# First chunks of the four sequences as one group with the decay in the mask, layer 1 opened on three of them, and squares moved to ScalarE

## The chip, the cores and the metric

The kernel runs on one core of a Trainium2 chip. The metric is the device time in microseconds (us) of one execution, of which a profile records the span from the first to the last instruction. Most executions of one kernel agree within about 0.3%, but some run with a lower granted TensorE clock in the records. So runs marked slow are left out of the ratios.

Engine names as in the profile: PE is TensorE, PEld its weight loads (they overlap PE), DVE is VectorE, ACT is ScalarE, POOL is GpSimd (here it issues the loads and scales v), SP is SyncE. A name with a q, such as POOLq, is the engine's sequencer.

## The reference

A decayed linear attention is followed by a feed-forward layer. There are 4 sequences of 768 positions, 8 heads of width 64, model width 512 and hidden width 2048; inputs are float32.

```python
gamma = 1.0 - 2.0 ** (-5.0 - np.arange(H))          # one decay per head
for t in range(S):
    state = gamma * state + outer(k[:, :, t], v[:, :, t])
    y[:, :, t] = scale * (q[:, :, t] @ state)
x = y.transpose(0, 2, 1, 3).reshape(B * S, H * D)   # 3072 x 512
h = x @ w_in                                        # layer 1
g = h + sin(alpha * h) ** 2 / (alpha + 1e-9)
out = g @ w_out                                     # layer 2
```

## The kernel before

Positions are cut into 24 chunks of 128, six per sequence. A chunk's attention has three stages. T transposes q and k on PE and copies them out of PSUM. A makes the scores and multiplies them by a 0/1 mask. M makes the values: for the first chunk of a sequence from the scores alone, for later ones also from a running state, which M updates too. The decay is taken out of the scores: v is scaled by a growing factor per position (`kg`), and the result by a falling one (`qg`, one table per chunk position, made by `decay_table`).

Chunks are put in groups for the feed-forward layer. Layer 1 has 16 slices per group: 4 matmuls, a sine on ScalarE, a square on ScalarE ("A") or VectorE ("D"), and on VectorE the sum `g`, which frees the slice's PSUM bank. A phase weaves layer 1 of one group with layer 2 of the group before and the attention of the group after.

```python
groups = [3, 2, 4, 4, 4, 4, 3]                 # chunks in the order of the sequences
def stage_T(j):
    open_T(j); half_T(j, 0); half_T(j, 1)      # 8 transposes on PE
    nc.scalar.copy(st["qkT", j], st["pt", j])  # 128x1024 from PSUM, on ScalarE
def stage_A(j):
    ...                                        # 8 matmuls into pa
    nc.vector.tensor_mul(aT, pa, mask_bc)      # 128x1024
def stage_M(j):
    ...                                        # state part (c > 0), value part, state update
    nc.vector.tensor_mul(xT[g][:, :, o:o + C], py, qg[:, c])
    ...                                        # two ScalarE copies of the state
def ff_in(g, f, square):
    ph = psum.tile([128, n], F32, tag="mm", bufs=4)
    ...                                        # 4 matmuls
    nc.scalar.activation(out=s, in_=ph, func=Sin, scale=alpha_sb[:, f:f + 1])
    ...                                        # square on ScalarE or VectorE
    return lambda: nc.vector.scalar_tensor_tensor(gT[g][:, f, :], s, rec_alpha[:, f:f + 1], ph, ...)

phase(0, [], {2: [G(3)], 5: [G(4)], 9: [T(3), V(3)], 11: [A(3)], 13: [G(5)]}, "AAD")
...                                            # chunk 4, and part of layer 2 of group 0
phase(1, outs[8:], {7: [T(5), V(5)], ...}, "AAAD")
for g in range(2, NG):
    ...
    phase(g, out_pieces(g - 1), att, "AAD" if g == 2 else "AAAD")
```

All loads but alpha and the first q and k go through one queue on POOL, in the order chunk 0 (v), 1, 2, three w_in pieces, chunk 3, w_in, chunk 4, four w_out pieces, then the other chunks. `idle_work` are matmuls on zeros, put where PE has nothing to do and meant to keep its clock up.

## Time and profile before

The kernel took 234.36 us in the median of 3 runs (234.17 to 234.95). The profiled execution spans 233.0 us.

These lines are from the page of the kernel before: the busy times (us, share of the span, instructions), the shares of the chain of waits, and two groups of instructions (out<-in, shapes, count | busy us, mean ns of one | idle us before it).

```profile
span 233.0 us, 4372 instructions
PE 214.8 (92%) x1737; PEld 113.8 (49%) x1766; DVE 146.8 (63%) x233; ACT 167.9 (72%) x297; POOL 84.4 (36%) x99
...
PE 72%; DVE 16%; ACT 7%; issue 3%; DVEq 0%; ACTq 0%
...
L224 DVE TENSOR_TENSOR s<-s 128x512 f32<-128x512 f32 (+2 forms) x30 | 19.5, 651 | 9.4 <-ACT s L220 9.4
...
L161 ACT COPY qkT<-pt 128x1024 bf16<-128x1024 bf16 x21 | 21.0, 1000 | 0.7 <-PE pt L154 0.7
```

PE is the bound over the span, but not everywhere. The timeline of PE of the kernel before (start us, duration us, then what it waited for in brackets) shows where layer 1 of groups 0, 1 and 2 starts:

```profile
17.45 3.55 PE L217 MATMUL ph<-xT,w_in 128*128 128x384 bf16 x20 [0.24 <-DVE xT L202]
...
39.26 0.60 PE L217 MATMUL ph<-xT,w_in 128*128 128x256 bf16 x4 [0.66 <-DVE xT L202]
...
64.55 1.02 PE L217 MATMUL ph<-xT,w_in 128*128 128x512 bf16 x3 [0.81 <-DVE xT L202]
```

And this is the busy time of the engines in two stretches of the kernel before (columns: stretch, its length, busy us of PE, PEld, DVE, ACT and POOL with instructions, granted clock, DMA engines' share, GB/s):

```profile
24.00:39.00 15.00, 11.02 (x121) 6.52 (x121) 13.50 (x23) 11.28 (x22) 6.83 (x9) 1.00 1.59 192
...
94.00:228.00 134.00, 131.96 (x954) 67.02 (x970) 75.59 (x103) 96.68 (x160) 7.30 (x8) 1.00 0.19 44
```

From 94 us on PE is 98% busy (131.96 of 134.00), and a shorter operation elsewhere can win next to nothing. From 24 to 39 us VectorE is 90% busy and PE 73%.

### The profile page before, as it was taken

The numbers are of one execution on the slowest core, as the hardware profiler recorded it, in microseconds if no ns is written. First come the engines' busy times: TensorE is split into PE (matmuls) and PEld (weight loads), VectorE is DVE, ScalarE is ACT, GpSimd is POOL, SyncE is SP. The second block draws the span as 40 slices with busy tenths as digits, with TensorE's granted clock in tenths as the row PEclk, the third lists the DMA queues.
The fourth block names the chain that finished last, engine by engine and source line by source line (L and its number), as shares of the span: only waits on it lengthen the run. The fifth ranks groups of instructions, "written<-read, shape, count | busy, mean of one in ns | idle before, by whom it ended". The sixth has DMA issues, their size and how long they took to land.

```text
span 233.0 us, 4372 instructions
## 1 busy us (share of the span) xinstructions
PE 214.8 (92%) x1737; PEld 113.8 (49%) x1766; DVE 146.8 (63%) x233; ACT 167.9 (72%) x297; POOL 84.4 (36%) x99
## 2 busy tenths in 40 slices
PE   7998867988889998999999999999999999999992
PEld 3554435555545454445555454455445545555440
DVE  6695996578846799646656656576557575445400
ACT  5478984787868886787787786786787876777420
POOL 8964734987999999930000000000000000000000
PEclk9999999999999999999999999999999999999998
DMA  9999999999999999970110110110111011111111
GB/s 131 141 197 184 184 207 171 155 150 184 114 153 108 111 147 113 141 88 3 48 45 0 48 45 1 48 45 1 48 45 45 3 45 45 48 45 45 45 71 67
DMA packets 82612, 20.48 MB, mean 88 GB/s; under 512 B 75408, under 2 KB 79520, under 8 KB 82592
## 3 DMA queue, kind: packets, MB, share of 16 engines
q0 software_dynamic: 77024, 13.37, 76.4%
q1 hardware_dynamic: 5568, 6.83, 8.5%
q8 instruction: 14, 0.23, 0.4%
q14 instruction: 6, 0.05, 0.1%
HBM read 27.27 MB, written 6.29 MB: 144 GB/s over the span
## 4 chain that ended last, share of the span: by engine, by line
PE 72%; DVE 16%; ACT 7%; issue 3%; DVEq 0%; ACTq 0%
PE po L234 31%; PE ph L217 27%; DVE aT L172 5%; DVE gT L225 4%; PE scratch L274 4%; ACT s L220 3%; PE pt L154 3%; PE pa L169 3%; DVE xT L202 3%; ACT qkT L161 3%; DVE s L224 2%; PE py L186 2%; PE py L190 2%; ACT s L222 1%; DVE qg L130 1%
## 5 line engine op out<-in xcount | busy, mean ns | idle before, releaser
L225 DVE SCALAR_TENSOR_TENSOR gT<-s,rec_alpha,ph 128x512 bf16<-128x512 f32 (+2 forms) x112 | 74.2, 669 | 52.3 <-ACT s L222 51.2
L217 PE MATMUL ph<-xT,w_in 128*128 128x512 bf16 (+2 forms) x444 | 99.5, 348 | 6.0 <-DVE gT L225 3.5
L234 PE MATMUL po<-w_out,gT 128*128 128x512 bf16 x361 | 95.4, 379 | 2.2 <-issue 1.4
L220 ACT ACTIVATE s<-ph,alpha_sb 128x512 f32<-128x512 f32 (+2 forms) x112 | 69.8, 626 | 36.1 <-PE ph L217 35.0
L217 PEld LDWEIGHTS <-w_in 128*128 128x128 bf16 x448 | 43.6, 98 | 51.6 <-issue 8.7
L234 PEld LDWEIGHTS <-gT 128*128 128x128 bf16 x384 | 34.7, 98 | 33.4 <-issue 0.5
L222 ACT ACTIVATE s<-s 128x512 f32<-128x512 f32 (+2 forms) x82 | 46.6, 568 | 2.6
L172 DVE TENSOR_TENSOR aT<-pa,mask 128x1024 bf16<-128x1024 f32 x24 | 29.3, 1222 | 6.7 <-PE pa L169 6.6
L224 DVE TENSOR_TENSOR s<-s 128x512 f32<-128x512 f32 (+2 forms) x30 | 19.5, 651 | 9.4 <-ACT s L220 9.4
L71 POOL DMA_DIRECT2D vr<-in_v_dram x24 | 21.9, 913 | 3.9 <-DMA w_out<-in_moe_w_out_dram 1.7
L71 POOL DMA_DIRECT2D qr<-in_q_dram x23 | 21.3, 927 | 3.3 <-DMA w_out<-in_moe_w_out_dram 1.7
L71 POOL DMA_DIRECT2D kr<-in_k_dram x23 | 20.4, 889 | 4.7 <-DMA w_out<-in_moe_w_out_dram 3.2
L161 ACT COPY qkT<-pt 128x1024 bf16<-128x1024 bf16 x21 | 21.0, 1000 | 0.7 <-PE pt L154 0.7
L243 ACT COPY o_sb<-po 128x512 f32<-128x512 f32 x23 | 13.5, 590 | 8.1 <-PE po L234 8.1
L206 ACT CAST s_bd<-ps 64x256 bf16<-64x256 f32 x40 | 14.5, 363 | 5.6 <-PE ps L199 4.1
L202 DVE TENSOR_TENSOR xT<-py,qg 128x512 bf16<-128x512 f32 x24 | 16.3, 679 | 2.5 <-PE py L190 2.5
L146 POOL TENSOR_TENSOR vr<-vr,kg 128x512 bf16<-128x512 bf16 x15 | 16.2, 1083 | 3.9 <-ACT s L222 2.1
L274 PE MATMUL scratch<-warm 128*128 128x512 bf16 x35 | 11.5, 462 | 1.4 <-DVE warm L105 1.2
L169 PE MATMUL pa<-qkT 64*128 64x128 bf16 x192 | 9.5, 219 | 2.3 <-ACT qkT L161 2.0
L169 PEld LDWEIGHTS <-qkT 64*128 64x128 bf16 x192 | 5.4, 94 | 11.5 <-ACT qkT L161 5.7
L190 PE MATMUL py<-aT,vr 128*64 128x128 bf16 x192 | 9.5, 220 | 0.5 <-DVE xT L202 0.4
L154 PE MATMUL pt<-ident,qr 128*128 128x128 bf16 x92 | 8.9, 219 | 1.0 <-DVE xT L202 1.0
(53 smaller groups left out, 89.2 us busy)
## 6 DMA issues: line engine op xcount, KB each, us to landing
out_dram<-o_sb SPq DMA_DIRECT2D x24, 256.0 KB, 2.0
vr<-in_v_dram POOLq DMA_DIRECT2D x24, 128.0 KB, 5.3
qr<-in_q_dram POOLq DMA_DIRECT2D x23, 128.0 KB, 4.9
kr<-in_k_dram POOLq DMA_DIRECT2D x23, 128.0 KB, 5.1
w_in<-in_moe_w_in_dram POOLq DMA_DIRECT2D x4, 512.0 KB, 10.2
w_out<-in_moe_w_out_dram POOLq DMA_DIRECT2D x4, 512.0 KB, 12.1
q<-in_q_dram SPq DMA_DIRECT2D x1, 256.0 KB, 3.3
k<-in_k_dram SPq DMA_DIRECT2D x1, 256.0 KB, 4.1
```

The lines of the kernel that those rows point to most:

```text
L71: nc.gpsimd.dma_start(out=t, in_=chunk_of(src, j))
L161: nc.scalar.copy(st["qkT", j], st["pt", j])
L169: nc.tensor.matmul(pa[:, e, p, :], qkT[r, NP + p, :], qkT[r, p, :], start=(p == 0), stop=True, skip_group_check=True)
L172: nc.vector.tensor_mul(aT.rearrange("p e n t -> p (e n) t"), pa.rearrange("p e n t -> p (e n) t"), mask_bc)
L202: nc.vector.tensor_mul(xT[g][:, :, o:o + C], py, qg[:, c])
L217: nc.tensor.matmul(ph, w_in[:, i, f * 128:(f + 1) * 128], xT[g][:, i, :], start=(i == 0), stop=(i == KS - 1))
L220: nc.scalar.activation(out=s, in_=ph, func=ACTF.Sin, scale=alpha_sb[:, f:f + 1])
L222: nc.scalar.activation(out=s, in_=s, func=ACTF.Square)
L224: (nc.vector if square == "D" else nc.gpsimd).tensor_mul(s, s, s)
L225: return lambda: nc.vector.scalar_tensor_tensor(gT[g][:, f, :], s, rec_alpha[:, f:f + 1], ph, op0=ALU.mult, op1=ALU.add)
L234: nc.tensor.matmul(po[g, ts], gT[g][:, f, ts * C:(ts + 1) * C], w_out[:, f, :], start=(f == 0), stop=(f == FF - 1))
L274: nc.tensor.matmul(scratch[:, :w], warm[:, :128], warm[:, :w], start=True, stop=True)
```

## The change

The intent has four parts.

1. The first chunks of the four sequences (called e0 to e3 here) make up group 0. They need no state, and with the decay put into the mask (`dec`, eight exponentials and one product) also no scaled v and no `qg` before M: M ends in a plain ScalarE copy.
2. Layer 1 opens on three of them: the first 8 slices run on 384 columns, then e3 is worked in, the same 8 slices run on its 128 columns, and slices 8 to 15 run on all 512.
3. The order of the queue changes: e3 comes after the first two w_in pieces, and the w_out pieces, which all stood behind w_in and chunks 3 and 4, now alternate with the last two of w_in.
4. From phase 1 on, all squares go to ScalarE, and the transposed copies of all later chunks go from ScalarE to VectorE.

The diff, cut to its core:

```diff
-    groups = [3, 2, 4, 4, 4, 4, 3]
+    order = [b * NCH for b in range(B)]
+    order += [b * NCH + c for b in range(B) for c in range(1, NCH)]
+    sizes = [4, 2, 4, 4, 4, 4, 2]
 ...
+    load_chunk(0, "v"); load_chunk(order[1]); load_chunk(order[2])
+    load_w_in(0); load_w_in(1); load_chunk(order[3])
+    load_w_out(0); load_w_in(2); load_w_out(1); load_w_in(3); load_w_out(2); load_w_out(3)
 ...
+    for h in range(H):
+        nc.scalar.activation(out=dec[:, h % 2, h // 2, :], in_=tio, func=ACTF.Exp, scale=lng[h], bias=back[:, h:h + 1])
 ...
-        nc.scalar.copy(st["qkT", j], st["pt", j])
+        nc.vector.tensor_copy(st["qkT", j], st["pt", j])
 ...
+        if c == 0:
+            nc.scalar.copy(x, py)
+            return
 ...
+    n3, early = 3 * C, 8
+    for f in range(early):
+        ff_in(0, f, "AAD"[f % 3], (0, n3))()
+    half_T(e3, 0, nc.scalar); idle_work(2); half_T(e3, 1, nc.vector); idle_work(4)
+    stage_A(e3)
+    decay_table(1); scale_v(e0, nc.vector); idle_work(4)
+    for f in range(4):
+        ff_out(0, 0, f)
+    stage_M(e3); idle_work(3)
+    for f in range(early):
+        ff_in(0, f, "AD"[f % 2], (n3, 4 * C))()
+    for t in s_bd:
+        nc.vector.memset(t, 0.0)
+    phase(0, [...], {9: [G(2)], 10: [G(3)], 12: [G(4)], 14: [G(5)]}, "AAD", range(early, FF))
 ...
-        phase(g, out_pieces(g - 1), att, "AAD" if g == 2 else "AAAD")
+        phase(g, out_pieces(g - 1, range(sizes[g - 1])), att, "A")
```

## The prediction

> **What bounds it now.** The chain of waits is 72% PE; PE is busy 92% of the 233.0 us span. Busy PE is not useful PE, so I count columns: a 512-column matmul runs every 0.216 us, a 384-column one every 0.162 us; one chunk's attention costs PE about 1.46 us (transposes 0.44, scores 0.33, state product 0.25, value product 0.22, state update 0.22). Useful work sums to about 199 us (estimate); the lost 34 us lie, by the timeline: 13.3 us before the first layer-1 matmul (17.45 us), 6.8 up to 39.3 (phase 0), 4.3 up to 64.6 (phase 1), 2.2 in phase 2, about 2.3 in the PE-bound rest, 4.1 after the last matmul (228.8). The change touches only what comes before the rest; it moves almost no PE work, so only those losses count.
>
> **Head.** It removes the v scaling, the state products and both state copies from the first three chunks, but adds eight exponentials (0.32 us each) and a 1.22 us mask product. ScalarE then carries copies, qg (4 x 0.32), the 1.28 us table load and the last x copy (0.6). First layer-1 matmul: 15.9 us instead of 17.45. It cannot be much earlier: POOL's waits show the first w_in piece landing near 15.6, and its place in the queue is unchanged.
>
> **Phase 0, the doubtful part.** Eight slices on three chunks are ScalarE-bound (1.03 us with the square there, 0.52 without): done near 24. The fourth chunk then runs serially (copy, scores, 1.22 us mask, values, copy): its layer 1 starts near 28.5, with ScalarE and PE nearly idle. Eight 128-column slices cost VectorE about 0.49 us each (estimate 0.34 per g, 0.30 per square): to 33.5. The last eight slices have 512 columns: VectorE pays 8 x 0.70, three squares 0.68, four decay tables 0.68 and two memsets 0.55, about 11 us; last g near 44.6, and PE, done near 42, waits for it. In the data queue w_out3 lands near 36 (each weight piece 2.55 us, each chunk 2.6), so no weight is late.
>
> **Fill and phase 1.** From 45 to 57 dense PE work covers chunks 4 and 5. Transposed copies go to VectorE: the Trainium skill ("VectorE: DVE Perf Modes", "Why PSUM operands drop a tier") allows 2 elements a cycle for 16-bit data from PSUM, so I estimate 0.69 us against ScalarE's 1.00; no copy of this form is in the trace. Phase 1 (256 columns, four chunks' attention) is VectorE-bound: 16 x 0.45 + 4 x (0.69 + 1.22 + 0.68) = 17.6, ScalarE about 18 with every square; 18.7 us with coupling, against 14.5 of PE work. Phase 2 starts near 75.8 instead of 64.6, but with only 8.4 us more work done.
>
> **Rest.** All squares on ScalarE make it 26 us per 33 us phase: still hidden. PE work left 151 us, losses 4.4, tail 4.1: span 235.5.
>
> **Predicted:** 236.5 us (timed runs are 1.4 above the span), range 232 to 240; faster by over 2% 0.1, within 2% 0.76, slower 0.14.
>
> **What would show it.** First layer-1 matmul near 15.9; a stretch of 24 to 29 us with little useful PE; VectorE busy over 90% from 34 to 44 with PE waiting for g; phase 1 about 19 us with VectorE above 90%; PE over 97% after 100 us; transposed copies 0.69 us.
>
> **What would make it wrong.** A faster phase 0 (VectorE operations overlapping, the fourth chunk's chain hidden): up to 5 us better. Phase 2 with less waste since POOL and VectorE collide less (one 1.67 us square at 91 us). Worse: late weights or chunks, or all ScalarE squares delaying g in phases 1 and 2.

## The result

The changed kernel took 237.63 us in the median of 4 runs (237.24 to 238.37), against 234.66 us (234.17 to 235.37) for 4 runs of the kernel before. The ratio is 1.0128, with a 95% interval of 1.009 to 1.0167. Ratios here are the mean time of one kernel's fast runs over that of the other's in the same rounds, so not quite the ratio of the medians. The change is slower, by 1.3%, within the 2% that counts as the same. The profiled span went from 233.0 to 235.5 us.

The same parts of the page of the changed kernel; the squares on VectorE are down to nine, and are not among the larger groups any more:

```profile
span 235.5 us, 4500 instructions
PE 214.7 (91%) x1769; PEld 115.2 (49%) x1798; DVE 142.7 (61%) x233; ACT 168.1 (71%) x327; POOL 92.6 (39%) x107
...
PE 64%; POOL 17%; DMA 12%; DVE 2%; issue 2%; ACT 1%; POOLq 0%
...
L190 DVE COPY qkT<-pt 128x1024 bf16<-128x1024 bf16 x20 | 13.8, 689 | 7.9 <-PE pt L180 7.5
```

Two things are to be seen. The transposed copy fell from 1000 ns on ScalarE to 689 ns on VectorE. And the chain of waits now puts 29% on POOL and on loads, which had no such share before. That is a strong hint, and the experiments show that it misleads.

The starts of layer 1 of groups 0, 1 and 2 in the timeline of PE of the changed kernel:

```profile
15.69 2.11 PE L258 MATMUL ph<-xT,w_in 128*128 128x384 bf16 x12
...
59.20 0.60 PE L258 MATMUL ph<-xT,w_in 128*128 128x256 bf16 x4
...
77.09 1.02 PE L258 MATMUL ph<-xT,w_in 128*128 128x512 bf16 x4 [0.33 <-DVE xT L243]
```

At the third of these the two kernels can be compared, but not directly: the changed kernel has one more chunk done by then. A chunk is 64 matmuls of 128 columns in layer 1 (3.46 us at the pace of 0.216 us per 512 columns), 16 matmuls of 512 columns in layer 2 (3.46 us), and 0.99 us of transposes, scores and values. In turn its order has put off one state product and one state update: counted in the traces, 48 and 56 matmuls of these stand before that point, against 56 and 64 in the kernel before, which is 0.47 us less. That makes 7.4 us more done (estimate; the prediction says 8.4). So:

| | before | changed | difference |
|---|---|---|---|
| layer 1 of group 0 starts, us | 17.45 | 15.69 | -1.8 |
| layer 1 of group 2 starts, us | 64.55 | 77.09 | +12.5, with 7.4 more done: 5.1 lost |
| from there to the end, us | 168.45 | 158.4 | -10.0, with 7.4 less to do: 2.6 won |
| span, us | 233.0 | 235.5 | +2.5 |

The changed kernel starts layer 1 of group 0 1.8 us earlier, as meant, and still arrives 5.1 us late at group 2. Where it loses is in the busy times by stretch of the changed kernel (columns as above):

```profile
24.00:29.00 5.00, 4.36 (x36) 2.00 (x35) 3.47 (x5) 1.15 (x3) 1.75 (x2) 1.00 1.24 206
29.00:34.00 5.00, 3.28 (x36) 2.30 (x35) 3.24 (x11) 3.86 (x13) 1.75 (x2) 1.00 1.34 202
34.00:46.00 12.00, 9.28 (x41) 3.74 (x40) 11.57 (x19) 8.31 (x13) 9.85 (x11) 1.00 2.15 137
46.00:59.00 13.00, 12.47 (x128) 6.71 (x132) 5.69 (x7) 3.92 (x9) 13.00 (x15) 1.00 1.83 150
59.00:77.00 18.00, 15.42 (x230) 11.99 (x232) 15.64 (x28) 15.67 (x41) 18.00 (x20) 1.00 1.47 106
```

The first row looks well used by PE, and isn't: most of it is matmuls on zeros (2.73 of the 4.36 us). This is e3's chain in the timeline of the changed kernel:

```profile
24.13 0.57 ACT L183 COPY qkT<-pt 128x512 bf16<-128x512 bf16 x1
...
24.75 0.38 PE L180 MATMUL pt<-ident,kr 128*128 128x128 bf16 x4 [0.65 <-ACT qkT L183]
24.97 1.03 PE L297 MATMUL scratch<-warm 128*128 128x512 bf16 x4
...
25.24 0.42 DVE L185 COPY qkT<-pt 128x512 bf16<-128x512 bf16 x1 [0.37 <-PE pt L180]
...
26.37 1.23 DVE L202 TENSOR_TENSOR aT<-pa,dec 128x1024 bf16<-128x1024 f32 x1 [0.70 <-PE pa L198]
...
28.55 0.58 ACT L240 CAST xT<-py 128x512 bf16<-128x512 f32 x1 [3.85 <-PE py L236]
...
29.18 0.83 PE L258 MATMUL ph<-xT,w_in 128*128 128x128 bf16 x12
```

For 5 us each step waits for the one before, and ScalarE idles 3.85 us. Then the eight 128-column slices come, which hold VectorE for 0.35 us each in `g` alone, and from 34 to 46 us the rest of phase 0, in which VectorE is busy 11.57 of 12.00 us. Its end in the same timeline:

```profile
42.14 1.07 POOL L107 TENSOR_TENSOR vr<-vr,kg 128x512 bf16<-128x512 bf16 x1
42.66 1.99 DVE L264 TENSOR_TENSOR s<-s 128x512 f32<-128x512 f32 x1
...
44.57 0.68 DVE L158 TENSOR_TENSOR qg<-qg,step 128x512 f32<-128x512 f32 x1
...
45.17 1.39 DVE L265 SCALAR_TENSOR_TENSOR gT<-s,rec_alpha,ph 128x512 bf16<-128x512 f32 x2
...
45.97 0.39 PE L275 MATMUL po<-w_out,gT 128*128 128x512 bf16 x1 [2.37 <-DVE gT L265]
```

PE waits 2.37 us for `g`. Ahead of the last two sums on VectorE stand a square that took 1.99 us instead of its usual 0.68, beside a scaling of v on POOL, and the last decay table.

### The profile page after: what moved, and what is told of

Its sections match the earlier page's. It is cut to its first block, busy times and chain, and to the rows that moved or that the text cites. A ratio compares the mean times of both kernels' runs of the same rounds, so it can differ in the third digit from the quotient of the medians.

```text
span 235.5 us, 4500 instructions
## 1 busy us (share of the span) xinstructions
PE 214.7 (91%) x1769; PEld 115.2 (49%) x1798; DVE 142.7 (61%) x233; ACT 168.1 (71%) x327; POOL 92.6 (39%) x107
## 4 chain that ended last, share of the span: by engine, by line
PE 64%; POOL 17%; DMA 12%; DVE 2%; issue 2%; ACT 1%; POOLq 0%
PE po L275 29%; PE ph L258 26%; DMA vr<-in_v_dram 6%; POOL vr L107 5%; DMA w_out<-in_moe_w_out_dram 4%; POOL vr L78 4%; POOL qr L78 4%; POOL kr L78 4%; PE pt L180 3%; PE py L232 2%; PE pa L198 2%; PE py L236 1%; DMA kr<-in_k_dram 1%; DVE aT L202 1%; DVE xT L243 1%
## 5 line engine op out<-in xcount | busy, mean ns | idle before, releaser
L265 DVE SCALAR_TENSOR_TENSOR gT<-s,rec_alpha,ph 128x512 bf16<-128x512 f32 (+3 forms) x120 | 76.1, 638 | 62.8 <-ACT s L262 62.1
L258 PE MATMUL ph<-xT,w_in 128*128 128x512 bf16 (+3 forms) x477 | 100.8, 336 | 4.8 <-DVE gT L265 4.1
L260 ACT ACTIVATE s<-ph,alpha_sb 128x512 f32<-128x512 f32 (+3 forms) x120 | 71.8, 599 | 35.7 <-PE ph L258 35.5
L262 ACT ACTIVATE s<-s 128x512 f32<-128x512 f32 (+3 forms) x111 | 61.1, 551 | 3.5
L275 PEld LDWEIGHTS <-gT 128*128 128x128 bf16 x384 | 35.1, 98 | 36.8 <-DVE gT L265 3.4
L107 POOL TENSOR_TENSOR vr<-vr,kg 128x512 bf16<-128x512 bf16 x23 | 25.0, 1099 | 2.7 <-DMA vr<-in_v_dram 2.7
L202 DVE TENSOR_TENSOR aT<-pa,mask 128x1024 bf16<-128x1024 f32 x20 | 24.4, 1222 | 2.2 <-PE pa L198 2.2
L190 DVE COPY qkT<-pt 128x1024 bf16<-128x1024 bf16 x20 | 13.8, 689 | 7.9 <-PE pt L180 7.5
L243 DVE TENSOR_TENSOR xT<-py,qg 128x512 bf16<-128x512 f32 x20 | 13.7, 684 | 2.3 <-PE py L236 2.2
L180 PE MATMUL pt<-ident,kr 128*128 128x128 bf16 x92 | 8.9, 219 | 1.3 <-ACT qkT L183 1.3
L180 PEld LDWEIGHTS <-qr 128*128 128x128 bf16 x92 | 6.9, 98 | 5.8 <-issue 1.7
```

Of the source, the lines that this page charges most:

```text
L107: eng.tensor_mul(raw["v", j], raw["v", j], kg[:, j % NCH, :, None].to_broadcast([128, H, D]))
L180: nc.tensor.transpose(pt[:, i * NP + p, :], raw["qk"[i], j][:, 2 * p:2 * p + 2, :].rearrange("p h d -> p (h d)"), ident)
L202: nc.vector.tensor_mul(aT.rearrange("p e n t -> p (e n) t"), pa.rearrange("p e n t -> p (e n) t"), m)
L243: nc.vector.tensor_mul(x, py, qg[:, c])
L258: nc.tensor.matmul(ph, w_in[:, i, f * 128:(f + 1) * 128], xT[g][:, i, lo:hi], start=(i == 0), stop=(i == KS - 1))
L260: nc.scalar.activation(out=s, in_=ph, func=ACTF.Sin, scale=alpha_sb[:, f:f + 1])
```

## The experiments

The theory, V: the time is lost in phase 0, to VectorE's stretch of 34 to 46 us and to e3's serial chain. There are two rivals. Q: it is lost on POOL and its load queue, as the chain of waits says (eight scalings of v more on POOL than before, 23 against 15, and loads behind them). S: it is lost to the squares, which ScalarE can't keep up with in phases 1 and 2.

### One: decay tables early

The four decay tables leave the full stretch for the time before layer 1 starts.

```diff
     nc.vector.reciprocal(rec_alpha, rec_alpha)
+    for c in range(2, NCH):
+        decay_table(c)
 ...
-          {9: [G(2)], 10: [G(3)], 12: [G(4)], 14: [G(5)]}, "AAD", range(early, FF))
+          {}, "AAD", range(early, FF))
```

> Edit: the changed kernel with its four decay tables 2 to 5 moved from the last eight slices of phase 0 to just before its first slice, where VectorE idles 2.9 us; same work, same order elsewhere. Theory V (VectorE's 34 to 46.6 us stretch delays everything after it): the last g of group 0 comes at about 43.9 instead of 46.6, phase 1 starts near 56.6, phase 2 near 74.5, time 237.6 - 2.6 = 235.0 us. Rival theory Q (the queue of chunk loads and v scalings on POOL, 29% of the chain after the change, holds phase 1): last g 43.9 too, but phase 1 waits longer for the q and k loads of its chunks and phase 2 still starts near 76.5 to 77, so the time stays at 237.0 to 237.6.

Measured: 236.09 us in the median of 4 runs (235.38 to 236.94), ratio to the kernel before 1.0061 (0.9994 to 1.0129). The two faster runs have a clock of 0.999 to 1.0, the two slower ones 0.991. The profiled span is 233.6 us, 1.9 less than the changed kernel's, both at full clock. The end of phase 0 in its timeline:

```profile
42.44 0.70 DVE L264 TENSOR_TENSOR s<-s 128x512 f32<-128x512 f32 x1
...
43.17 1.53 DVE L265 SCALAR_TENSOR_TENSOR gT<-s,rec_alpha,ph 128x512 bf16<-128x512 f32 x2
...
43.98 0.39 PE L275 MATMUL po<-w_out,gT 128*128 128x512 bf16 x1 [1.00 <-DVE gT L265]
```

The last `g` ends at 44.70 instead of 46.56 us, 1.9 earlier, and the whole of that arrives at the end of the kernel. So VectorE's stretch is on the critical path, as V says. The timed runs alone would not show it: the ratio's interval overlaps that of the change (1.009 to 1.0167).

The edit took more off that stretch than the 2.7 us of four tables. The square that took 1.99 us beside POOL's scaling takes 0.70 us here, since it now starts at 42.44, just before that scaling ends (41.50 to 42.58). So about 4 us went and 1.9 us arrived; what the tables and what the missed collision gave is not separated. With both gone, VectorE waits for squares of ScalarE now and then (0.49 us ahead of a sum at 41.77).

### Two and three: POOL relieved

Three of the 23 scalings of v go from POOL to VectorE, at moments when VectorE has room; once in the changed kernel and once on top of the early tables.

```diff
-        if n in (11, 13, 15):
-            scale_v(order[(n - 9) // 2], nc.gpsimd)
 ...
+    scale_v(e1, nc.vector)
     stage_M(P[5])
 ...
+        if g < 4:
+            att.setdefault(8, []).append(V((e2, e3)[g - 2]))
         phase(g, out_pieces(g - 1, range(sizes[g - 1])), att, "A")
```

> Edit: the changed kernel with three v scalings (1.07 us each on POOL, chunks 0 of sequences 1 to 3) moved to VectorE, into stretches where it has room. Theory V: PE's waits for loads in phase 1 were 0.7 us in all, so at most 0.7 us is gained: 236.9 to 237.6. Theory Q: phase 2 starts 1 to 2 us sooner and the time falls to 235.5 to 236.5.

> Edit: the two edits together. Theory V alone: no more than the early tables alone give, 235.0. Theory Q alone: as the POOL relief alone, 236. If both chains run close to each other, only this run gets the whole gain: 234.3 to 235.0, with the early tables alone stuck in between.

Measured: alone 237.92 us in the median (236.12 to 238.22), ratio 1.0112 (1.0028 to 1.0196); with the early tables 235.54 us (235.39 to 236.36), ratio 1.0043 (0.9988 to 1.0099). The profiled run of the first had the granted clock at 0.50 from 33.6 to 37.0 us, before the edit acts, and stays 0.8 to 1.0 us behind the changed kernel from there to the end. The second is the clean comparison: its profiled span is 233.6 us, as with the early tables alone, and the first and last `g` of every group start within 0.1 us of that kernel's. Freeing POOL of three scalings is worth nothing. Q falls, as far as these three go: the other five that the change put on POOL stayed there.

Why, then, did the chain of waits name POOL and loads? This is where it enters them, in the timeline of the changed kernel:

```profile
70.41 0.68 DVE L243 TENSOR_TENSOR xT<-py,qg 128x512 bf16<-128x512 f32 x1
...
71.15 0.38 PE L180 MATMUL pt<-ident,qr 128*128 128x128 bf16 x4 [0.52 <-DMA kr<-in_k_dram]
```

The transposes write the PSUM tile that `xT` has to leave first (both have the tag `ty`, with one buffer). `xT` ends at 71.09 and the transposes start at 71.15. The k of this chunk, the tenth in the order, was issued at 47.74 us and had landed by 53.05. The load that the chain takes is another one, issued at 68.13 us for a later chunk, which landed at 72.37, after the transposes had started; it signals on a semaphore that they wait on too. The wait ended with VectorE, and the inference from semaphores picked that load. Followed back from there, the chain runs along POOL to the head of the kernel. It has no such branch in the profile of the early tables, where POOL's share of the chain is 0% with the same POOL work.

### Four: squares back on VectorE

A part of the squares goes back to VectorE, in the pattern of the kernel before: "AAAD" in phase 1 and from phase 3 on, "AAD" in phase 2.

```diff
-          ... 15: [M(P[9])]}, "A")
+          ... 15: [M(P[9])]}, "AAAD")
 ...
-        phase(g, ..., att, "A")
+        phase(g, ..., att, "AAD" if g == 2 else "AAAD")
```

> Edit: the changed kernel with the squares shared between ScalarE and VectorE again (in group 1 and from group 3 on one slice in four on VectorE, in group 2 one in three), as before the change. Rival theory S (all squares on ScalarE delay g, that is where the 3 us went): time falls by 1 to 3 us to 234.6 to 236.6. Theory V: ScalarE has 26 us of work in a 33 us phase, so nothing is gained; 237.2 to 239, slower where POOL and VectorE collide again in phases 1 and 2.

Measured: 241.48 us in the median of 4 runs, of which two are slow (241.78 and 243.12, clock 0.993); the fast ones are 237.99 (clock 0.999) and 241.18 (clock 0.992). The ratio of the fast runs, 1.0209 (1.0064 to 1.0354), is unclear. Only stretches at full clock are used. From the first `g` of group 1 to that of group 2 it took 20.8 us, against 18.6 in the changed kernel, and from there to that of group 3 28.6 against 27.7. After that the two run equally. Both stretches had a granted clock of 1.00. So the squares on ScalarE win about 3 us by these stretches, and S falls in its sign. Where the 3 us went can be read in the same stretches: two squares of 256 columns took 1.34 and 0.98 us instead of 0.42, and two of 512 columns 1.51 and 1.57 us instead of 0.69, each beside a scaling of v on POOL. That is 3.2 us over their usual time, the collision that the expectation named; no run takes it away by itself. Single fast runs do not show that whole gain (237.99 against 237.24 at the best), and I leave the size of it open.

### Five and six: no opening on three chunks

The second part of the change is undone: layer 1 waits for all four chunks and runs 16 slices of 512 columns. This takes the eight 128-column slices away, and e3's chain from the middle of phase 0. The second version also loads e3 ahead of w_in.

```diff
-    n3, early = 3 * C, 8
-    for f in range(early):
-        ff_in(0, f, "AAD"[f % 3], (0, n3))()
-    half_T(e3, 0, nc.scalar)
+    half_T(e3, 0, nc.vector)
 ...
-    for f in range(early):
-        ff_in(0, f, "AD"[f % 2], (n3, 4 * C))()
 ...
+    phase(0, [], {}, "AAD", range(4))
+    phase(0, [lambda f=f: ff_out(0, 0, f) for f in range(FF - 4)],
+          {9: [G(2)], 10: [G(3)], 12: [G(4)], 14: [G(5)]}, "AAD", range(4, FF))
     # second version only:
     load_chunk(order[2])
+    load_chunk(order[3])
     load_w_in(0); load_w_in(1)
-    load_chunk(order[3])
```

> Edit: the changed kernel without the opening on three chunks: the fourth chunk's attention runs in the head, then layer 1 of group 0 goes in 16 slices of 512 columns instead of 8 of 384, 8 of 128 and 8 of 512; loads in the same order. Theory V (the serial fourth chunk and 24 VectorE slices in place of 16 are the loss): layer 1 starts only when the fourth chunk's v has landed, near 23 us instead of 15.7, and still its last g comes near 43.5 instead of 46.6; time 237.6 - 2.7 = 235 us. Rival H (the early start at 15.7 is worth what it saves, the loss is elsewhere): time rises with the start, to 241 or more.

> Edit: as unsplit, and the fourth chunk's loads stand before the first two w_in pieces in the queue. Theory V: all four chunks are there near 15.6, w_in near 18.2; layer 1 starts near 18.4, last g near 38.5, time near 230 us. Rival H: 237 or more.

Measured: 236.92 us (236.63 to 239.03; ratio 1.0102, 1.0041 to 1.0163) and 232.14 us (231.76 to 234.19; ratio 0.9892, 0.984 to 0.9943). Both missed by about 2 us on the high side. These are the first layer-1 matmuls of the two, the last square on VectorE and the last two sums, from their timelines, the first version and then the second:

```profile
24.32 4.48 PE L258 MATMUL ph<-xT,w_in 128*128 128x512 bf16 x20
...
43.08 1.76 DVE L264 TENSOR_TENSOR s<-s 128x512 f32<-128x512 f32 x1
...
45.36 1.39 DVE L265 SCALAR_TENSOR_TENSOR gT<-s,rec_alpha,ph 128x512 bf16<-128x512 f32 x2
```

```profile
20.30 4.04 PE L258 MATMUL ph<-xT,w_in 128*128 128x512 bf16 x18
...
38.86 0.69 DVE L264 TENSOR_TENSOR s<-s 128x512 f32<-128x512 f32 x1
...
40.07 1.46 DVE L265 SCALAR_TENSOR_TENSOR gT<-s,rec_alpha,ph 128x512 bf16<-128x512 f32 x2
```

The first version starts layer 1 8.6 us later than the changed kernel (24.32 instead of 15.69) and starts its last `g` at 46.0 us, against 45.8. So the early start, which was the point of opening on three chunks, is worth nothing: what it wins is given back in e3's chain and in the double set of sums. The second version starts 4.0 us earlier than the first, and its last `g` moves from 46.0 to 40.8 us. The place of e3 in the queue, behind w_in, was most of what held the first version back: PE waits 2.90 us there for e3's q, up to 18.66 us, and starts the same transposes at 15.60 in the second version. Two other things add to the 5.2 us. The first version's profiled run had the granted clock at 0.50 from 18.2 to 21.6 us, after that wait, which made e3's chain about 1 us longer (5.66 us from there to layer 1, against 4.70). And its last square took 1.76 us beside a scaling of v on POOL, against 0.69 in the second. The second version keeps the opening undone, so an opening on three with e3 ahead of w_in is not tested.

### Seven and eight: early tables and more squares on VectorE, without the opening

Here the tables are made before layer 1 on top of the second version, and then the squares of phase 0 are also set to "AD".

```diff
     nc.vector.reciprocal(rec_alpha, rec_alpha)
+    for c in range(2, NCH):
+        decay_table(c)
 ...
-    phase(0, [...], {9: [G(2)], 10: [G(3)], 12: [G(4)], 14: [G(5)]}, "AAD", range(4, FF))
+    phase(0, [...], {}, "AAD", range(4, FF))       # eighth run: "AD"
```

> Edit: as unsplit_queue, with decay tables 2 to 5 before the first slice. Theory V: VectorE has 14.6 us and ScalarE 17.6 us of work for the 16 slices, so ScalarE bounds: last g near 37.5, time near 229.3 us, about 0.7 below unsplit_queue. If the phase is PE-bound by then: no gain.

> Edit: as unsplit_tables, with the squares of group 0 alternating between ScalarE and VectorE (8 to 8 instead of 11 to 5). ScalarE 15.9 us, VectorE 16.6 us: if ScalarE bounded unsplit_tables, 0.5 to 1 us less: near 228.5 us; if not, the same or slower.

Measured: 232.29 us (232.28 to 233.11; ratio 0.9889, 0.9856 to 0.9922) and 233.23 us (232.93 to 233.54; ratio 0.992, 0.989 to 0.9951). Neither gained on 232.14, and both expectations were missed. In VectorE's timeline of the seventh run the tables stand ahead of e3's first copy:

```profile
14.98 2.43 DVE L158 TENSOR_TENSOR qg<-qg,step 128x512 f32<-128x512 f32 x4
17.33 0.42 DVE L185 COPY qkT<-pt 128x512 bf16<-128x512 bf16 x1
```

The tables stood on VectorE from 15.0 to 17.4 us, ahead of e3's copies, and put the start of layer 1 off to 21.6 us from 20.30; what was won at the end of the stretch was lost at its start. With "AD" the last `g` starts at 41.5 us, 0.2 later than without. From 24 to 42 us ScalarE was the busier of the two without "AD" (15.66 of 18.00 us, VectorE 14.80); with it VectorE is (16.76, ScalarE 13.80), so the bound changed sides. One of its squares also took 1.23 us beside a scaling on POOL, 0.55 more than usual, so whether "AD" would gain without that stays open. Of the 1.2 us by which its profiled span is longer (231.7 against 230.5), 1.0 comes after the last `g` of the kernel.

### Nine: everything in its place

The version that follows from the above: the two halves of e3's transposes stand before and after M of e2; the tables come after e3's mask product, while PE makes its values and ScalarE copies them out; the scaling of e0's v and the memsets come after the last `g`.

```diff
     stage_A(e2)
+    idle_work(3)
+    half_T(e3, 0, nc.vector)
     nc.vector.tensor_scalar_add(rec_alpha, alpha_sb, 1e-9)
     nc.vector.reciprocal(rec_alpha, rec_alpha)
-    idle_work(5)
     stage_M(e2)
+    half_T(e3, 1, nc.vector)
     idle_work(3)
+    stage_A(e3)
+    for c in range(1, NCH):
+        decay_table(c)
+    idle_work(5)
+    stage_M(e3)
 ...
+    phase(0, [], {}, "AAD", range(4))
+    phase(0, [...], {}, "AAD", range(4, FF))
+    scale_v(e0, nc.vector)
+    for t in s_bd:
+        nc.vector.memset(t, 0.0)
```

> Edit: as unsplit_queue, but the fourth chunk's transposes stand among the third chunk's steps, all decay tables stand behind the fourth chunk's mask (where VectorE waits 2 to 3 us for the first sine), and the v scaling and the two memsets stand behind the last g. In unsplit_tables the early tables held up the fourth chunk's copies on VectorE and moved the start from 20.3 to 21.6, which ate the gain. Theory V: layer 1 starts near 19.0, ScalarE bounds the 16 slices, last g near 39.4 instead of 40.8 to 41.5; time near 230.3 us, 2 below unsplit_queue. If PE or the loads bound the head: start stays at 20 and the time at 231.5 to 232.

Measured: 230.38 us in the median of 6 runs (230.28 to 231.33; clocks 0.996 to 0.999), ratio to the kernel before 0.983 (0.979 to 0.9871). It beats the kernel before by 1.7% (by the 2% rule this is unclear, between faster and the same), and the change as given by about 3% (0.983 over 1.0128). The profiled span is 229.5 us. Two lines of its timeline, the first layer-1 matmul and PE's wait for the second-to-last `g`:

```profile
19.77 4.48 PE L258 MATMUL ph<-xT,w_in 128*128 128x512 bf16 x20
...
39.59 0.39 PE L275 MATMUL po<-w_out,gT 128*128 128x512 bf16 x1 [0.89 <-DVE gT L265]
```

Layer 1 of group 2 starts at 70.31 us, against 77.09 in the changed kernel with the same work done: 6.8 us earlier. The last `g` of the kernel keeps all of that (its end at 218.24 against 225.02 us) and the span 6.0: the rest goes behind the last ScalarE copy, where this run took 4.1 us to its end and the changed kernel 3.3.

### Ten: six groups of four

With four chunks in group 0, all groups can have four: `sizes = [4] * 6`. There is then no phase with 256 columns. The attention of group 1 must be done between phases 0 and 1, so the fifth chunk's transposes move into slot 12 of phase 0.

```diff
-    sizes = [4, 2, 4, 4, 4, 4, 2]
+    sizes = [4] * 6
 ...
+    phase(0, [...], {9: [V(e0)], 10: [memsets], 12: [T(P[4])], 14: [A(P[4]), SK(P[0])]}, "AAD", range(4, FF))
+    for i in (4, 5, 6):
+        stage_T(P[i + 1]); fill(3); stage_A(P[i + 1]); stage_M(P[i]); fill(3)
+    fill(3); stage_M(P[7]); fill(3)
-    phase(1, ...)
-    for g in range(2, NG):
+    for g in range(1, NG):
```

> Edit: as unsplit_tuned, with six groups of four chunks in place of 4, 2, 4, 4, 4, 4, 2; the attention of chunks 4 to 7 moves between the output matmuls of group 0, 28 of which are left for phase 1. Reason: phase 1 had 14.5 us of PE work in 17.9 us since VectorE pays for four chunks' attention beside it. With 25.7 us of PE work against 26 of ScalarE it should lose about 1 us instead of 3.4. Time near 228.5 us; if ScalarE in phase 1 binds harder than counted, 230 or more.

Measured: 235.53 us in the median of 6 runs (231.9 to 235.93), a miss. Four of the six count as slow (clock 0.983 to 0.985); of the two others one has a clock of 0.999 and took 231.9 us, the other 0.981 and 234.78. The ratio of the fast runs, 0.9945 (0.985 to 1.0039), says little. Its profile is of a slow run, and is read here only for what lowered the clock. Two lines of PE in its timeline, and then the stretch that follows (the clock is the third number from the end of that row):

```profile
36.99 0.61 PE L180 MATMUL pt<-ident,qr 128*128 128x128 bf16 x4 [3.03 <-DMA qr<-in_q_dram]
...
38.86 1.91 PE L258 MATMUL ph<-xT,w_in 128*128 128x512 bf16 x4
```

```profile
38.00:46.00 8.00, 7.97 (x46) 3.55 (x46) 4.43 (x6) 3.70 (x7) 7.07 (x9) 0.65 2.02 128
```

The fifth chunk's q lands near 37 us, and PE stands for 3.03 us before its transposes. Soon after, four matmuls of 512 columns take 1.91 us where they take 1.02 us at full clock; the granted clock is 0.50 from 36.8 to about 43.6 us (a mean of 0.65 over these 8 us is 5.6 us at 0.50 and the rest at 1.00). The Trainium skill ("TensorE: Matmul & The Clock Gate", "What's actually happening") has a clock gate with two levels, half and full, that goes by how busy PE has recently been; this trace agrees, with 0.50 after a wait of 3.03 us. The half clock lasted 6.6 us from the first matmul after the wait, so this wait cost 3.03 us of its own and, by my estimate from the half pace, about 3 us more in slow matmuls. One of six runs kept a clock of 0.999, and was 1.5 us slower than the median of run nine even so; it has no profile, and that remainder is open.

## Why the prediction was right, and where its parts were off

The time predicted was 236.5 us (232 to 240), within 2% with a chance of 0.76; measured were 237.63 us and a ratio of 1.0128. The span came out at 235.5 us as predicted, and that exactness is luck: layer 1 of group 2 started 1.3 us later than said (77.09 against 75.8) and the rest took 1.1 us less (158.4 against 159.5). The steps, point by point:

- **Head: right.** 15.9 us was predicted for the first layer-1 matmul, and 15.69 measured, right behind the last copy of x on ScalarE (15.05 to 15.64). The side remark was off: the first w_in piece had landed at 14.1 us, not near 15.6.
- **e3's chain: right.** Layer 1 on it was put at 28.5 and began at 29.18 us; the useful work of PE in 24 to 29 us was small, as said. The 128-column `g` took 0.347 us against the 0.34 estimated.
- **VectorE above 90% from 34 to 44 us, with PE waiting for `g`: right in kind, 2 us too small.** VectorE was 96% busy from 34 to 46 us and PE waited 2.37 us, but the last `g` ended at 46.56, not near 44.6. The term that was mis-sized is "three squares 0.68": one of them took 1.99 us beside POOL's work. That alone is 1.3 us; 0.7 us more came from the later start of the 128-column slices (29.18 against 28.5). The prediction had named such a collision (a square of 1.67 us in the kernel before, 1.75 us in its timeline), but for a later phase, as one that might get rarer.
- **Phase 1: right in time, wrong in reason.** 18.7 us was predicted and 17.9 measured (59.20 to 77.09). VectorE was not above 90% busy; it was at 87% (15.64 of 18.00 us), with ScalarE at 87% too. That the chunks' own chain filled the rest is likely and not tested.
- **Transposed copies: right.** The Trainium skill ("VectorE: DVE Perf Modes", "Why PSUM operands drop a tier") was the ground for 0.69 us, and the trace shows 689 ns for all 20.
- **Rest: right.** 159.5 us was predicted from layer 1 of group 2 on (151 + 4.4 + 4.1), and 158.4 measured; PE is 99% busy from 105 to 230 us (123.31 of 125.00). Squares on ScalarE stayed hidden, and run four says that they help in phases 1 and 2.
- **Time above the span: off by 0.3.** The prediction added 1.4 us by taking one run's span from another set's median. The profiled runs themselves are 1.9 (before) and 1.7 us (changed) above their spans.

The prediction came to the right total, but did not say what the opening on three is worth, and that is why the change does not win: the 1.8 us won at the head buys nothing, since what comes after is bound by VectorE and by e3's chain. The fifth run shows it: layer 1 starts 8.6 us later, and the last `g` comes at the same time. The group of first chunks can pay: with e3 ahead of the weights and no opening on three it did, by 1.1% in the sixth run and 1.7% in the ninth. The other parts of the change, the decay in the mask and the transposed copies on VectorE, were never undone by themselves, so their share is not known.

## What to carry to other kernels

An early start of the bounding engine is worth only what the stage after it can take: before one splits work to start sooner, one should sum what the split adds to the engine that ends that stage. The small jobs that can stand anywhere (tables, memsets, scalings) belong where the engine that does them is idle, and one should look on both sides of the place, since a job ahead of a dependent chain delays it (here 2.4 us of tables put it off by 1.3 us). A chain of waits that suddenly goes through loads should be checked by whether the named load is the one needed and when that one landed, and by taking the named work away.

## What the Trainium skill lacked or had wrong

- "SBUF — State Buffer", "Who interferes with whom": it says that a VectorE instruction with two SBUF inputs and a GpSimd instruction that reads SBUF block each other for a whole instruction. The trace agrees in kind: a square that takes 0.68 us alone took 1.99 us beside a scaling of v on POOL. But that scaling ended 0.55 us after the square's start (42.66 to 43.21), so the lock on it accounts for 0.55 of the 1.31 us more; 0.76 us is left for which the page gives no cause, and no run here settled it. The profile's spans on POOL are rough, so this split is an estimate. In the fourth run three squares fit the lock (0.98, 1.51 and 1.57 us, longer by 0.56, 0.82 and 0.88 with 0.69, 0.95 and 1.01 us of overlap).
- "ScalarE: Activation LUTs", "What ACT_TABLE_LOAD costs": 1283 ns for the load agrees (1.28 us at 2.49 and at 13.64 us). The drain of about 1380 ns that the page adds does not show in the changed kernel: the second load starts 0.02 us after the instruction before it ends (13.46 + 0.16), and the next instructions start at 3.79 and at 14.94 us, 0.02 us after each load ends. The switch from Exp to Sin cost 1.3 us in this trace and not 2.7.
- "TensorE: Matmul & The Clock Gate", "What's actually happening": its table lets the clock fall after one idle window of about 3.4 us and come back after about 3.4 us of sustained work. The length agrees: the clock was at 0.50 for 3.4 us in the profiles of the second, fourth and fifth run (33.6 to 37.0, 46.2 to 49.6 and 18.2 to 21.6 us), and for twice that, 6.8 us, in the tenth. But the 3.4 us before the fall were not wholly idle: PE was busy in them for 1.91, 1.11, 0.96 and 0.56 us. The profile of the changed kernel had PE busy for 1.92 us in the same stretch as the second run (30.2 to 33.6 us), and its clock stayed at 1.00.
- No page that I read warns that the releaser which a profile infers for a wait can be wrong. Here it put 29% of the chain of waits on POOL and loads, and taking three of POOL's scalings away changed the span by 0.0 us (233.6 and 233.6).
